# Eight PSUM banks as one tile in place of four tiles of two banks, in a fused attention and phase-mixing kernel

## The chip, the cores and the metric

The kernel runs on one core of a Trainium2 chip. The metric is the device time of one execution in microseconds. Five queues run side by side, each in its own order: PE (TensorE, matrix multiplications and transposes into PSUM), DVE (VectorE), ACT (ScalarE), POOL (GpSimd, here elementwise work in SBUF and DMA issue) and SP (SyncE, here DMA issue). They are kept in step by semaphores: an instruction waits until the counters of other engines and of DMAs have reached certain values. PSUM has eight banks of 512 float32 per partition.

## The reference

Inputs are q, k and v of shape (4, 8, 768, 64) and four matrices. Attention is causal; heads 0, 2 and 6 see all earlier keys, the other five see the first four keys and a window of 64. Its output x (768 x 512 per batch element) goes through a phase mixing over the sequence and a channel step:

```
scores = where(mask, q @ k.T / 8, -1e9);  a = softmax(scores);  x = a @ v      # heads side by side
theta = x @ w_theta
y = w_tok_r @ (x * cos(theta)) + w_tok_i @ (x * sin(theta))
u = x + y
out = u + max(u @ w_ch, 0)
```

## The kernel before

The whole program is one list of steps, `ORDER`, written out by hand; no scheduler moves anything. A step such as `mx.1.3.0.0` names a helper and its arguments, and each helper issues its instructions on a fixed engine (or the one that the letter D, A or P at the end of the step names). Each engine runs its part of the list in list order. The waits between engines are placed by the tile framework when the program is built, from the tiles and parts of tiles that each instruction reads and writes.

Work goes by batch element (first argument), in 128-row tiles of the sequence, and steps of two or three batch elements are interleaved. The steps, with the PSUM banks that they use as their last number:

- `lf`, `lq`, `lv`, `lt`, `lw` load q and k, v, the token matrices and the two weights; q, k and the token matrices go by POOL's queue, v and the first q and k by SP's.
- `tq` turns a pair of heads of q or k on PE into one bank (lines 252 and 255), and `eq` copies it out to SBUF by ACT (line 259) or DVE (line 261). `xp`/`xe` do the same for x, `wt`/`we` for the token matrices (line 437), `up`/`ue` for u (line 423).
- `pm` puts the additive mask into one or two banks (lines 290, 294), `s` adds the scores (line 319), `e` takes the exponential of both banks in one ACT instruction (line 349, or 346 for one bank), and `m` masks by multiplication on DVE (lines 359 to 371).
- `av` multiplies with the values into two banks (line 406), `n` normalises both (lines 411, 413).
- `th` makes theta for two row tiles in two banks (line 446), `tr` takes cosine and sine of both (lines 450, 451), `z` multiplies with x on DVE or POOL (lines 458, 459).
- `mx` accumulates a third of the token mixing of one row tile in one bank (line 463, 4 matmuls; three steps fill the bank), `u` adds x to it on DVE (line 469).
- `xd` and `ud` transpose x and u by DMA from SP's queue (line 418), `ch` multiplies u with w_ch into one bank (line 473), `o` is the last step on DVE (line 476), `st` stores. `w` issues matmuls whose result nobody reads (line 432).

The eight banks are numbered 0 to 7. They are held by four tiles of two banks each; bank b is half b % 2 of tile b // 2, so that 0 and 1, 2 and 3, 4 and 5, 6 and 7 share a tile. `one(bank)` gives one bank, `two(bank)` a pair that starts with an even number:

```
    def one(bank):
        return banks[bank // 2][:, bank % 2]

    def two(bank):
        return banks[bank // 2]
```

Of the kernel before, what the change touches and what calls it, by code (L numbers as in the profile page):

```python
# [8 lines left out]
F32 = mybir.dt.float32  # L9
# [99 lines left out]
def kernel(ctx: ExitStack, tc: tile.TileContext, q, k, v, is_retrieval, n_sink, window, w_theta, w_tok_r, w_tok_i, w_ch, out):  # L109
# [9 lines left out]
    psum = ctx.enter_context(tc.tile_pool(name="psum", bufs=1, space=bass.MemoryType.PSUM))  # L119
    ctx.enter_context(tc.manual_schedule())  # L120

    def new(name, shape, dtype=BF16):
        return sb.tile(shape, dtype, name=name)
# [24 lines left out]
    u, uT = [new(f"u{n}", [128, DM]) for n in range(U_BUFS)], [new(f"uT{n}", [128, KD, 128]) for n in range(U_BUFS)]  # L148
    ot = [new(f"ot{n}", [128, DM], F32) for n in range(OT_BUFS)]
    rr = [new(f"rr{n}", [128, 8], F32) for n in range(2)]  # L150
    banks = [psum.tile([128, 2, 512], F32, name=f"bank{n}") for n in range(4)]

    def one(bank):
        return banks[bank // 2][:, bank % 2]
# [405 lines left out]
```

## Time and profile before

| | us |
|---|---|
| median of 3 runs | 195.82 |
| the three runs | 193.15, 195.82, 196.24 |
| the profiled execution | 194.51 |
| its span, first to last instruction | 192.8 |
| PE busy | 171.1 |
| DVE busy | 138.1 |
| ACT busy | 114.0 |
| POOL busy | 59.3 |

The profile is that of one execution. Busy times are those of each engine's own work; weight loads of PE (PEld) run beside its matmuls. In a timeline row the bracket at the end gives how long the engine was idle before the row and whose work ended that: "0.71 <-DVE u L469" is 0.71 us until DVE's instruction of line 469, which writes u, had finished. The names leave buffer numbers out, so which bank a row works on is read from the list of steps. Line numbers are those of the kernel before.

### The profile page before, as it was taken

The page shows a single profiled execution, that of the slowest core. Times are in us where ns is not written, and L with a number is a line of the kernel's source. Part 1 is how long each engine was busy: PE and PEld are TensorE (multiplying, and loading weights), DVE is VectorE, ACT ScalarE, POOL GpSimd, SP SyncE. Part 2 cuts the span into 40 slices and gives each one's busy share as a digit, 9 for nine tenths or more (in the row PEclk, how much of TensorE's full clock was granted, in tenths as well). Part 3 has the DMA queues.
Part 4 walks back from the last instruction along what each step waited for, and adds up shares of the span by engine and source line. Part 5 has one row for each costly group of instructions (what it writes and reads, how often), then busy time and mean ns, then how long its engine had stood idle before and what let it go on. Part 6 is the DMA issues. An engine that isn't in the chain of part 4 may idle for free.

```text
span 192.8 us, 4430 instructions
## 1 busy us (share of the span) xinstructions
PE 171.1 (89%) x1821; PEld 95.6 (50%) x1821; DVE 138.1 (72%) x253; ACT 114.0 (59%) x132; POOL 59.3 (31%) x99
## 2 busy tenths in 40 slices
PE   5585978999898999989989989998899999998970
PEld 5353466755554476534445665443346644443430
DVE  4523854999687975689979988999778838825442
ACT  4596799899888908468997036788653066100000
POOL 7314954626254504351822316160000000400000
PEclk9889999999999999999999999999999999999999
DMA  5998899945999989699899998851421555116454
GB/s 169 259 203 186 121 200 200 203 89 83 155 195 185 186 121 136 135 156 238 103 181 220 141 192 146 195 137 27 126 95 27 114 107 136 54 58 196 130 199 154
DMA packets 62227, 28.72 MB, mean 149 GB/s; under 512 B 48384, under 2 KB 59136, under 8 KB 62208
## 3 DMA queue, kind: packets, MB, share of 16 engines
q1 hardware_dynamic: 51808, 19.54, 46.7%
q0 software_dynamic: 10400, 8.92, 32.1%
q8 instruction: 14, 0.23, 0.5%
q14 instruction: 5, 0.04, 0.1%
HBM read 25.69 MB, written 6.29 MB: 166 GB/s over the span
## 4 chain that ended last, share of the span: by engine, by line
PE 64%; DVE 20%; ACT 9%; DMA 2%; issue 2%; DVEq 0%; SPq 0%
PE bank L463 28%; PE bank L473 10%; PE bank L446 8%; PE bank L319 5%; PE bank L406 5%; DVE ot L476 4%; PE bank L255 3%; DVE qT L261 3%; ACT P L349 3%; DVE kT L261 3%; DVE u L469 3%; DMA early<-in_k_dram 2%; DVE early L458 2%; PE bank L437 2%; ACT kT L259 1%
## 5 line engine op out<-in xcount | busy, mean ns | idle before, releaser
L349 ACT ACTIVATE P<-bank 128x1024 bf16<-128x1024 f32 (+2 forms) x64 | 56.8, 944 | 9.2 <-PE bank L319 8.6
L463 PE MATMUL bank<-zr,wtokTr 128*128 128x512 bf16 x72 | 27.3, 379 | 2.1 <-DVE u L469 1.2
L463 PE MATMUL bank<-early,wtokTr 128*128 128x512 bf16 x72 | 27.3, 379 | 1.5 <-DVE u L469 0.9
L463 PE MATMUL bank<-early,wtokTi 128*128 128x512 bf16 x72 | 27.3, 379 | 0.0
L463 PE MATMUL bank<-zi,wtokTi 128*128 128x512 bf16 x72 | 27.3, 379 | 0.0
L473 PE MATMUL bank<-w_ch_sb,uT 128*128 128x512 bf16 x96 | 24.0, 379 | 1.3 <-DVE ot L476 0.6
L463 PEld LDWEIGHTS <-wtokTi 128*128 128x128 bf16 x144 | 14.0, 98 | 17.6 <-issue 4.7
L463 PEld LDWEIGHTS <-wtokTr 128*128 128x128 bf16 x144 | 14.0, 97 | 16.9 <-issue 2.4
L476 DVE SCALAR_TENSOR_TENSOR ot<-bank,u 128x512 f32<-128x512 f32 x24 | 16.0, 685 | 6.4 <-PE bank L473 4.3
L319 PE MATMUL bank<-qT,kT 64*128 64x128 bf16 (+2 forms) x240 | 20.0, 256 | 0.2 <-ACT kT L259 0.2
L450 ACT ACTIVATE ct<-bank,half_pi 128x1024 f32<-128x1024 f32 x12 | 13.4, 1115 | 10.2 <-PE bank L446 8.0
L406 PEld LDWEIGHTS <-P 128*128 128x128 bf16 x472 | 16.6, 97 | 4.9 <-issue 1.5
L261 POOL CAST vt<-st_v 128x512 bf16<-128x512 f32 x12 | 9.8, 823 | 27.1 <-DMA st_v<-in_v_dram 26.3
L406 PE MATMUL bank<-vt,P 128*128 128x65 bf16 x372 | 16.9, 193 | 1.1 <-ACT P L349 1.0
L371 DVE TENSOR_TENSOR P<-P,m_stream 128x1024 bf16<-128x1024 bf16 (+3 forms) x27 | 14.3, 557 | 2.6 <-ACT P L349 2.6
L458 POOL TENSOR_TENSOR early<-early,st 128x512 bf16<-128x512 bf16 x3 | 3.4, 1160 | 41.5 <-issue 35.7
L473 PEld LDWEIGHTS <-uT 128*128 128x128 bf16 x96 | 9.1, 97 | 11.9 <-issue 2.1
L319 PEld LDWEIGHTS <-kT 64*128 64x128 bf16 x240 | 11.0, 96 | 7.5 <-issue 5.9
L469 DVE TENSOR_TENSOR u<-early,bank 128x512 bf16<-128x512 bf16 x12 | 8.1, 683 | 8.4 <-PE bank L463 7.0
L261 DVE COPY qT<-bank 128x768 bf16<-128x768 bf16 x9 | 8.4, 951 | 6.8 <-PE bank L255 3.0
L261 POOL COPY kO<-kT 128x320 bf16<-128x320 bf16 (+3 forms) x18 | 5.3, 322 | 23.0 <-DVE kT L261 14.1
L451 ACT ACTIVATE st<-bank 128x1024 f32<-128x1024 f32 x12 | 12.2, 1018 | 0.0
(90 smaller groups left out, 293.8 us busy)
## 6 DMA issues: line engine op xcount, KB each, us to landing
st_v<-in_v_dram SPq DMA_DIRECT2D x24, 256.0 KB, 6.9
out_dram<-ot SPq DMA_DIRECT2D x24, 256.0 KB, 2.3
qb<-in_q_dram POOLq DMA_DIRECT2D x14, 192.0 KB, 7.9
kb<-in_k_dram POOLq DMA_DIRECT2D x14, 192.0 KB, 7.8
wtok<-in_moe_w_tok_r_dram POOLq DMA_DIRECT2D x6, 192.0 KB, 6.3
wtok<-in_moe_w_tok_i_dram POOLq DMA_DIRECT2D x6, 192.0 KB, 6.4
early<-in_q_dram SPq DMA_DIRECT2D x2, 384.0 KB, 4.9
early<-in_k_dram SPq DMA_DIRECT2D x2, 384.0 KB, 5.9
```

Source lines behind the costliest of these rows:

```text
L261: (nc.vector if eng == "D" else nc.gpsimd).tensor_copy(o, i)
L319: nc.tensor.matmul(*mms[g], start=not seeded, stop=True, skip_group_check=True)
L349: nc.scalar.activation(o, two(bank)[:, :, :o.shape[2]], AF.Exp, scale=scale)
L371: nc.vector.tensor_tensor(o, o, mk, ALU.mult)
L406: nc.tensor.matmul(o, l, r, start=(m == 0), stop=True, skip_group_check=True)
L446: nc.tensor.matmul(two(bank)[:, y], xT[b % 2][:, kk, i * 128:(i + 1) * 128], w_theta_sb[:, kk], start=(kk == 0), stop=(kk == KD - 1))
L450: nc.scalar.activation(ct[n], two(bank), AF.Sin, bias=half_pi)
L451: nc.scalar.activation(st[n], two(bank), AF.Sin)
L463: nc.tensor.matmul(one(bank), wtokT[n][:, s, t * 128:(t + 1) * 128], z[b % 2][:, s], start=(s == 0 and n == 0), stop=(s == NB - 1 and n == ...
L469: nc.vector.tensor_tensor(u[ui(b, t)], x[b % 2][:, t], one(bank), ALU.add)
L473: nc.tensor.matmul(one(bank), uT[ui(b, t)][:, kk], w_ch_sb[:, kk], start=(kk == 0), stop=(kk == KD - 1))
L476: nc.vector.scalar_tensor_tensor(ot[(NB * b + t) % OT_BUFS], one(bank), 0.0, u[ui(b, t)], ALU.max, ALU.add)
```

## The change

One tile of eight banks is allocated, and the four names are views of two banks each. Addresses, shapes, the list of steps and every instruction stay as they are:

```
-    banks = [psum.tile([128, 2, 512], F32, name=f"bank{n}") for n in range(4)]
+    big = psum.tile([128, 8, 512], F32, name="big")
+    banks = [big[:, 2 * n:2 * n + 2] for n in range(4)]
```

What moves is where the framework puts waits. In the program built from the kernel before, 79 of the waits between engines name an instruction that touches only the other bank of the same tile (28 where DVE waits for PE, 20 PE for DVE, 17 between ACT and PE, 14 between ACT and DVE). In the program of the changed kernel there is none: every wait for PSUM names an instruction on the same bank. What an instruction is sure to come after is in no place more than before. Written out, the waits on other engines and on DMAs are PE 304 before and 319 now, DVE 243 and 251, ACT 144 and 148, POOL 112 and 110, SP 159 and 158; the instructions that raise a counter are PE 183 and 190, DVE 205 and 213, ACT 122 and 128.

Two places in the built programs. A row is line, operation, out<-in and shape, with the counters that it waits for; `bank_128` is the tile of banks 0 and 1, `bank_130` that of 4 and 5. First PE in the third quarter of the program, the steps `tq.3.k.1.1`, `tq.3.k.3.4` and `tq.3.q.1.5`: before,

```order
L255 LDWEIGHTS kb
L255 MATMUL bank_128<-ident,kb 64x128 [waits Activation_49]
...
L255 LDWEIGHTS kb [waits DMASW7_49]
L255 MATMUL bank_130<-ident,kb 64x128 [waits Activation_49]
...
L255 LDWEIGHTS qb [waits DMASW6_49]
L255 MATMUL bank_130<-ident,qb 64x128
```

and now,

```order
L256 LDWEIGHTS kb
L256 MATMUL big<-ident,kb 64x128 [waits Activation_49]
...
L256 LDWEIGHTS kb [waits DMASW7_49]
L256 MATMUL big<-ident,kb 64x128 [waits DVE_49]
...
L256 LDWEIGHTS qb [waits DMASW6_49]
L256 MATMUL big<-ident,qb 64x128 [waits Activation_49]
```

The turn of k into bank 4 waited for ACT, which copies bank 5 out (`eq.3.q.0.5.A`), and the turn of q into bank 5 then needed no wait. Now the first waits for DVE, which copies bank 4 out (`eq.3.k.0.4.D`), and the second for ACT.

Second DVE at the end of the program, the steps `u.3.5.0` to `o.3.3.1`, all on the tile of banks 0 and 1 but one: before,

```order
L469 TENSOR_TENSOR u_115<-early_100,bank_128 128x512 [waits PE_49]
L261 COPY uT_121<-bank_128 128x512 [waits PE_49]
L476 SCALAR_TENSOR_TENSOR ot_122<-bank_128,u_112 128x512 [waits DMAHW5_49,DVE_49]
L476 SCALAR_TENSOR_TENSOR ot_124<-bank_129,u_114 128x512 [waits DMAHW7_49,DVE_49,PE_49]
L476 SCALAR_TENSOR_TENSOR ot_125<-bank_128,u_115 128x512 [waits DMAHW0_49,DVE_49,PE_49]
L476 SCALAR_TENSOR_TENSOR ot_123<-bank_128,u_113 128x512 [waits DMAHW2_49]
```

and now,

```order
L470 TENSOR_TENSOR u_115<-early_100,big 128x512 [waits PE_49]
L262 COPY uT_121<-big 128x512 [waits PE_49]
L477 SCALAR_TENSOR_TENSOR ot_122<-big,u_112 128x512 [waits DMAHW5_49,DVE_49]
L477 SCALAR_TENSOR_TENSOR ot_124<-big,u_114 128x512 [waits DMAHW7_49,DVE_49,PE_49]
L477 SCALAR_TENSOR_TENSOR ot_125<-big,u_115 128x512 [waits DMAHW0_49,DVE_49,PE_49]
L477 SCALAR_TENSOR_TENSOR ot_123<-big,u_113 128x512 [waits DMAHW2_49,PE_49]
```

The two last rows were both held by one wait for PE, in front of the first of them, for the last matmul of the program. Now each waits for PE on its own, the first for the matmuls of its own bank. The first row waits for PE as before, but for the mix in its own bank and no longer for the channel step in the other one, which the row can't show, since it leaves out the counter's value.

## The prediction

> **What bounds the kernel now.** First the page of the profiled execution: busy time, then the chain of work that ended last.
>
> ```profile
> span 192.8 us, 4430 instructions
> PE 171.1 (89%) x1821; PEld 95.6 (50%) x1821; DVE 138.1 (72%) x253; ACT 114.0 (59%) x132; POOL 59.3 (31%) x99
> PE 64%; DVE 20%; ACT 9%; DMA 2%; issue 2%; DVEq 0%; SPq 0%
> ```
>
> TensorE (PE) is busy for 171.1 of 192.8 us, yet only 64% of the chain is its: 20% runs through VectorE (DVE) and 9% through ScalarE (ACT). The chain changes engine wherever PE waits until a PSUM bank has been read, or a reader waits until PE has filled one. This execution took 194.51 us, 1.71 us more than its span and 0.7% below the median of 195.82 us. Then busy time by stage (columns: stretch, its length, then PE, PEld, DVE, ACT, POOL busy with counts, clock, DMA):
>
> ```profile
> 6.00:21.50 15.50, 10.88 (x146) 7.13 (x148) 5.84 (x17) 11.21 (x14) 5.72 (x13) 0.89 0.98 190
> 21.50:30.00 8.50, 7.27 (x133) 4.81 (x126) 5.32 (x14) 8.36 (x12) 5.88 (x9) 1.00 1.16 199
> 36.00:49.00 13.00, 12.36 (x162) 7.04 (x159) 12.59 (x16) 11.95 (x14) 6.61 (x8) 1.00 0.71 116
> 83.00:94.00 11.00, 10.56 (x78) 4.95 (x78) 10.33 (x14) 8.96 (x10) 4.48 (x6) 1.00 1.22 164
> 94.00:109.00 15.00, 14.40 (x185) 8.21 (x184) 13.45 (x34) 10.30 (x13) 5.64 (x9) 1.00 1.14 170
> 140.00:174.00 34.00, 34.00 (x273) 17.48 (x273) 22.73 (x44) 11.95 (x12) 2.28 (x2) 1.00 0.32 81
> ```
>
> From 140 to 174 us PE is never idle, from 21.5 to 30 ACT is full, from 36 to 49 DVE is: nothing that shortens waits pays much there. From 6 to 21.5 us no engine is full. They wait for each other, and the question for every such wait is whether the two instructions share a bank or only a tile.
>
> **The change, part by part.** No instruction is added, removed or moved, on any queue, and none grows. What goes are the 79 waits in which one engine waits for work on the other bank of a two-bank tile. No wait holds anything longer than in before, since each instruction is held by a subset of what held it. So the sum runs over stalls that such waits end, up to where the next wait ends last. Bank numbers are those of the order (last number of a step).
>
> *6 to 21.5 us.* Rows of the timeline (start, duration, engine, line, and in brackets the idle time before and what ended it):
>
> ```profile
> 7.44 0.49 PE L252 MATMUL bank<-ident,kb 128*128 128x128 bf16 x6 [2.07 <-ACT qT L259]
> 7.97 0.80 ACT L259 COPY kT<-bank 128x768 bf16<-128x768 bf16 x1 [0.58 <-PE bank L252]
> 10.33 0.82 PE L252 MATMUL bank<-ident,qb 128*128 128x128 bf16 x6
> 12.38 0.96 DVE L261 COPY qT<-bank 128x768 bf16<-128x768 bf16 x1 [2.58 <-PE bank L432]
> 13.38 0.55 PE L432 MATMUL bank<-ident 128*128 128x128 bf16 x7 [0.57 <-DVE qT L261]
> 15.39 0.22 PE L290 MATMUL bank<-n_causal,ident 128*128 128x128 bf16 x1 [0.79 <-DVE kT L261]
> 16.59 0.38 ACT L346 ACTIVATE P<-bank 128x256 bf16<-128x256 f32 x1 [1.79 <-PE bank L255]
> 17.71 0.86 PE L255 MATMUL bank<-ident,qb 128*64 128x128 bf16 x24 [0.84 <-ACT kT L259]
> 19.35 0.53 PE L255 MATMUL bank<-ident,kb 128*64 128x128 bf16 x12 [0.78 <-DVE qT L261]
> 20.26 1.02 ACT L349 ACTIVATE P<-bank 128x1024 bf16<-128x1024 f32 x1 [0.85 <-PE bank L319]
> ```
>
> All five PE rows with a bracket wait for the other bank: k.0's turn (bank 1) for the copy out of bank 0; `w.7.7` for the copy out of 6; the seed `pm.0.5.3` for 2; q.2's turn into 3 for 2; k.3's turn into 2 for 3. DVE's copy at 12.38 reads bank 6, whose turn ended at 10.33 + 0.82 = 11.15, and waits for warm-up matmuls in bank 7. ACT carries this stage into its full stretch, so I count on ACT. The first stall gives it 0.55 of its 0.58 us. The next two, in series on PE, give 0.57 + 0.79; with 0.55 that is 1.91, and ACT's row at 16.59 comes at 14.68, when ACT is indeed free (16.59 - 1.79 - 0.55 = 14.25). The last two free PE by 0.84 + 0.78, of which ACT can use its idle 0.85 at 20.26. Sum 1.91 + 0.85 = 2.8 us; at least 1.9, at most 0.58 + 1.79 + 0.85 = 3.2.
>
> The clock in this stage is not the change's, but the shorter pause might touch it:
>
> ```profile
> 8.83 1.57 PE L319 MATMUL bank<-qT,kT 64*128 64x256 bf16 x12 [0.20 <-ACT kT L259]
> 10.00:11.00 1.00, 1.00 (x10) 0.56 (x6) 0.00 (x0) 0.99 (x2) 0.54 (x1) 0.50 1.28 192
> ```
>
> PE had half its clock there (0.50), after the 2.07 us pause; I take the same again, 0. The Trainium skill ("TensorE: Matmul & The Clock Gate", What's actually happening) says that about 3.4 us with too little PE activity, in a free-running window, halve the clock. By that rule the pause, shorter by 0.70, may leave the clock up and the 12 matmuls might take half of 1.57 us: 0.8 us more saved. The trace agrees with a halved clock and can't show the window.
>
> *30 to 60 us.*
>
> ```profile
> 30.46 0.81 PE L446 MATMUL bank<-w_theta_sb,xT 128*128 128x512 bf16 x3 [0.49 <-DVE xT L261]
> 44.20 1.82 DVE L261 COPY qT<-bank 128x768 bf16<-128x768 bf16 x2 [0.38 <-ACT kT L259]
> 57.83 0.80 ACT L259 COPY wtokTr<-bank 128x768 bf16<-128x768 bf16 x1 [0.48 <-PE bank L437]
> 58.66 1.13 DVE L261 COPY wtokTi<-bank 128x768 bf16<-128x768 bf16 x2 [1.65 <-ACT wtokTr L259]
> ```
>
> Bank 2 of theta waits for a copy out of 3 (0.49); DVE as reader of one bank waits for ACT as reader of its neighbour at 44.20 (0.38) and 58.66, where it sits through ACT's copy of 0.80. Sum 1.6, all on the path; at least 0.8, because DVE has only 13.00 - 12.59 = 0.41 us to give from 36 to 49; at most 0.49 + 0.38 + 1.65 = 2.5.
>
> *60 to 140 us.*
>
> ```profile
> 72.68 0.38 PE L463 MATMUL bank<-zr,wtokTr 128*128 128x512 bf16 x1 [0.71 <-DVE u L469]
> 82.99 1.02 PE L473 MATMUL bank<-w_ch_sb,uT 128*128 128x512 bf16 x4 [0.52 <-DVE kT L261]
> 86.64 0.69 DVE L476 SCALAR_TENSOR_TENSOR ot<-bank,u 128x512 f32<-128x512 f32 x1 [0.67 <-PE bank L463]
> 100.08 0.38 PE L463 MATMUL bank<-early,wtokTr 128*128 128x512 bf16 x1 [0.60 <-DVE u L469]
> 113.49 0.53 PE L255 MATMUL bank<-ident,kb 128*64 128x128 bf16 x12 [0.88 <-ACT qT L259]
> 134.59 0.38 PE L463 MATMUL bank<-zr,wtokTr 128*128 128x512 bf16 x1 [0.47 <-DVE u L469]
> 138.32 0.69 DVE L476 SCALAR_TENSOR_TENSOR ot<-bank,u 128x512 f32<-128x512 f32 x1 [0.30 <-PE bank L463]
> 139.06 0.38 PE L463 MATMUL bank<-zr,wtokTr 128*128 128x512 bf16 x1 [0.78 <-DVE ot L476]
> ```
>
> PE at 72.68 fills bank 1 and waits for the reader of 0, at 82.99 the reverse: 0.71 + 0.52 = 1.2 us, at least 0.7. Then DVE is nearly full too (0.67 us free from 83 to 94). At 86.64 `o.0.5.0` waits for a mix in bank 1 and heads a run of DVE work; at 100.08 and 113.49 PE waits for the neighbour: 0.67 + 0.60 + 0.88 = 2.15. I take 2.0; at least 0.9 (the last stall alone), at most 2.2. From 132 on 0.47, and 0.30 of the 0.78: that wait stays, for `o.1.5.2` in the same bank, which itself loses only its 0.30 for bank 3: 0.8; at least 0.5, at most 0.47 + 0.78 = 1.25.
>
> *140 us to the end.*
>
> ```profile
> 175.21 0.38 PE L463 MATMUL bank<-early,wtokTr 128*128 128x512 bf16 x1 [0.49 <-DVE ot L476]
> 182.84 0.38 PE L463 MATMUL bank<-early,wtokTi 128*128 128x512 bf16 x1
> 184.12 0.69 DVE L469 TENSOR_TENSOR u<-early,bank 128x512 bf16<-128x512 bf16 x1 [1.11 <-PE bank L473]
> 184.86 0.40 PE L423 MATMUL bank<-ident,u 128*128 128x128 bf16 x4 [0.78 <-DVE u L469]
> 186.37 1.89 PE L473 MATMUL bank<-w_ch_sb,uT 128*128 128x512 bf16 x8 [0.25 <-DVE ot L476]
> 188.29 1.29 DVE L476 SCALAR_TENSOR_TENSOR ot<-bank,u 128x512 f32<-128x512 f32 x2 [1.38 <-PE bank L473]
> ```
>
> At 175.21 bank 1 waits for `o.2.3.0` (bank 0): 0.5. The add `u.3.5.0` needs the mix that ended at 182.84 + 0.38 = 183.22 and waits until 184.12 for `ch.3.2.1`: it starts 0.86 earlier, the turn behind it by 0.75 of PE's 0.78, `ch.3.5.0` by 0.25 more. At the very end both finishing adds wait for the last matmul; now the first (1.29 / 2 = 0.65) runs beside it: 0.6. Sum 1.6; at least 1.2, at most 1.8.
>
> *What comes in its place.* There are 27 more waits (PE 15, DVE 8, ACT 4). A hand-over takes 0.05 us (`u` ends at 184.81, the turn starts at 184.86), so at most 27 x 0.05 = 1.35; one that is already met should cost little: 0.3. Next late are the transposing DMAs, which PE's channel matmuls need:
>
> ```profile
> DMA to landing us min/median/max: 2.4/2.5/8.9
> ```
>
> Each starts earlier with its `u`, but where DMAs are dense (1.14 to 1.22 in the last column but one, 83 to 109 us) earlier work doesn't make them faster, and the longest took 6.4 us more than the median: 0.7. Together -1.0, between 0 and -3.
>
> The skill has a rule against the change as well: by the same page (The cost: per-tile semaphore tail) matmuls' semaphore increments serialize at about 26 ns each. PE gets 7 more signalling instructions: an estimate of 0.2 us, by which the saving below would be 9.3. No row here separates such a tail.
>
> *Sum.* 2.8 + 1.6 + 1.2 + 2.0 + 0.8 + 0.5 + 1.6 - 1.0 = 9.5 us: 194.51 - 9.5 = 185.0 for the profiled execution, and 195.82 / 194.51 of that, 186.3, for a median; I say **186 us**.
>
> **The rivals.**
>
> *Absorbed.* Only the two ends, where no engine is full, keep their gain, at its lower bounds: 1.9 + 1.2 = 3.1, so 191.4, or 192.7 as a median. For it: from 83 to 109 us PE and DVE are both over 89% busy, so one's gain meets the other's work. Against it: most stalls there sit on PE itself, which is on the path. Chance 0.12.
>
> *Slower.* From 83 to 117 us loads for the next batch, asked for earlier, run into the transposes of `u`, and PE stops at `ch`. One landing late by 8.9 - 2.5 = 6.4 us leaves 9.5 - 6.4 = 3.1 saved (192.7); three in series lose 19.2 and give 205.5. It decides beyond 9.5 + 3.9 = 13.4 us lost. Against it: the loads and the transposes move earlier together. Chance 0.03.
>
> *The change doesn't do what it says*: eight banks held as one, any reader waiting for any matmul. From 6 to 21.5 us alone, ACT and PE in turn would take 11.21 + 10.88 = 22.1 us in place of 15.5: over 201 us in all. The built program has no such wait: 0.
>
> **How the numbers follow.** The forecast has 0.85. All terms at their lower ends give 6.5 - 3 = 3.5, at their upper ends 12.7; not all err together, so 5.5 to 12.5, or 183.3 to 190.3 as medians. The three runs of before reach from 193.15 to 196.24, so a median may sit 1% lower still: 182 to 191. About 2% (3.9 us) is what a measurement here can tell from no change. Faster by more: the forecast less its low edge, 0.84; within: 0.13; slower: 0.03.
>
> **What would show it.** Right: the brackets above at 13.38, 72.68, 100.08 and 175.21 are gone; no add of L469 waits for a channel matmul of L473; ACT's full stretch begins about 2.8 us earlier; PE stays at about 171 us busy in a span near 183. Wrong: the same idle time in front of PE with other releasers (DMA, or readers of the same bank), or stalls that go while L473 waits for `uT` in their place.

## The result, and the profile after

| | before | after |
|---|---|---|
| median of 4 runs, us | 195.34 (193.15 to 196.24) | 185.87 (185.3 to 186.6) |
| profiled execution, us | 194.51 | 185.3 |
| its span, us | 192.8 | 183.3 |

After takes 0.9553 of the time of before (95% interval 0.9457 to 0.9649). Beside later kernels, on another chip, it took 187.78 us (186.16 to 188.66), 0.9631 of before (0.9557 to 0.9705); after's own median moves by 2 us between chips, so kernels are compared below within one chip where less than that matters. On some chips part of the executions of a kernel form a second group that is 1% to 3% slower; medians, ranges and ratios here and below are those of the faster group (the 187.96 us that an expectation quotes is the median of all).

The page of after (busy time; the chain that ended last; 25 of its 1821 matmul records are missing, so that PE's 166.9 is somewhat low):

```profile
span 183.3 us, 4404 instructions
PE 166.9 (91%) x1796; PEld 94.7 (52%) x1821; DVE 135.8 (74%) x253; ACT 113.3 (62%) x132; POOL 57.8 (32%) x99
PE 64%; DVE 12%; DMA 10%; ACT 8%; issue 2%; POOL 1%; SPq 1%; POOLq 0%; DVEq 0%
```

DVE's share of the chain fell from 20% to 12%, that of DMAs rose from 2% to 10%. The engines wait for each other less, and transfers have become what is late. By stage (same columns as before), with the cut 2.8 us earlier, at 18.70 in place of 21.50, where the forecast puts the start of ACT's full stretch:

```profile
6.00:18.70 12.70, 11.65 (x151) 7.50 (x152) 6.63 (x19) 11.40 (x15) 3.97 (x9) 1.00 1.09 218
18.70:27.00 8.30, 7.01 (x124) 4.77 (x124) 5.87 (x13) 8.18 (x13) 5.73 (x10) 1.00 1.02 156
```

ACT's instruction that starts at 21.54 in before starts at 17.91 here, so that the stretch begins 3.63 us earlier. The 1.00 in the clock column (third from the end) says little for the first microseconds: the clock records of this trace begin at 9.6 us, and the column shows 1.00 where there is none. The experiment with a seam comes back to this.

At the end, the add `u.3.5.0` (first row) no longer waits 1.11 us for a channel matmul but 0.17 us for its own mix, and three finishing adds run in a row where the last two used to wait 1.38 us for PE:

```profile
175.65 0.69 DVE L470 TENSOR_TENSOR u<-early,big 128x512 bf16<-128x512 bf16 x1 [0.17 <-PE big L464]
177.17 2.08 DVE L477 SCALAR_TENSOR_TENSOR ot<-big,u 128x512 f32<-128x512 f32 x3
179.42 0.69 DVE L477 SCALAR_TENSOR_TENSOR ot<-big,u 128x512 f32<-128x512 f32 x1 [0.17 <-PE big L474]
```

What has come in place of the old stalls stands in the waits of after (who <- for what: us in total, times, longest):

```profile
PEld L474 <- DMA uT<-u: 3.3, 3, 2.6
PEld L447 <- DMA xT<-x: 1.6, 1, 1.6
PE big L464 <- DVE wtokTi L262: 2.0, 1, 2.0
```

Since no instruction changed its place on an engine, the n-th weight load of PE (or the n-th instruction of ACT or DVE) is the same work in both traces. Start in before less start in after is the lead of after at that point:

| instruction | start before | start after | lead | since the row above |
|---|---|---|---|---|
| PE, scores (L319 before) | 24.13 | 20.50 | 3.63 | +3.63 |
| ACT, copy of kT | 43.37 | 38.58 | 4.79 | +1.16 |
| PE, scores | 45.75 | 43.09 | 2.66 | **-2.13** |
| PE, mix | 62.84 | 58.22 | 4.62 | +1.96 |
| ACT, sine | 86.79 | 80.51 | 6.28 | +1.66 |
| PE, mix | 88.03 | 83.81 | 4.22 | **-2.06** |
| PE, values | 104.84 | 99.81 | 5.03 | +0.81 |
| PE, values | 108.70 | 104.33 | 4.37 | **-0.66** |
| PE, theta | 120.44 | 114.35 | 6.09 | +1.72 |
| PE, mix | 125.37 | 120.55 | 4.82 | **-1.27** |
| PE, channel | 148.60 | 141.93 | 6.67 | +1.85 |
| PE, mix | 172.75 | 165.95 | 6.80 | +0.13 |
| PE, mix | 179.96 | 172.43 | 7.53 | +0.73 |
| DVE, last add | 188.90 | 179.42 | 9.48 | +1.95 |

The gains add up to 15.60 us, and 6.12 are given back at four places. The experiments ask three things: are the waits between banks the cause, do the gains of the stretches add, and what takes the 6 us back?

### The profile page after: what moved, and what is told of

The parts are those of the page before. It is cut to its first block, busy times and chain, and to the rows that moved or that the text cites. A ratio compares the mean times of both kernels' runs of the same rounds, so it can differ in the third digit from the quotient of the medians.

```text
span 183.3 us, 4404 instructions
## 1 busy us (share of the span) xinstructions
PE 166.9 (91%) x1796; PEld 94.7 (52%) x1821; DVE 135.8 (74%) x253; ACT 113.3 (62%) x132; POOL 57.8 (32%) x99
## 4 chain that ended last, share of the span: by engine, by line
PE 64%; DVE 12%; DMA 10%; ACT 8%; issue 2%; POOL 1%; SPq 1%; POOLq 0%; DVEq 0%
PE big L464 28%; PE big L474 9%; PE big L447 7%; PE big L320 6%; PE big L407 6%; DMA st_v<-in_v_dram 5%; ACT P L350 4%; DVE kT L262 3%; PE big L256 3%; DMA xT<-x 2%; DMA early<-in_k_dram 2%; PE big L438 2%; DVE qT L262 2%; DVE early L459 2%; DVE zr L459 1%
## 5 line engine op out<-in xcount | busy, mean ns | idle before, releaser
L350 ACT ACTIVATE P<-big 128x1024 bf16<-128x1024 f32 (+2 forms) x64 | 56.7, 947 | 9.5 <-PE big L320 8.6
L464 PE MATMUL big<-zi,wtokTi 128*128 128x512 bf16 x70 | 26.5, 379 | 0.8 <-issue 0.6
L464 PE MATMUL big<-early,wtokTi 128*128 128x512 bf16 x69 | 26.2, 379 | 0.3 <-issue 0.2
L464 PE MATMUL big<-early,wtokTr 128*128 128x512 bf16 x69 | 26.2, 380 | 0.2
L464 PE MATMUL big<-zr,wtokTr 128*128 128x512 bf16 x64 | 24.3, 380 | 2.1 <-DVE wtokTi L262 2.0
L474 PE MATMUL big<-w_ch_sb,uT 128*128 128x512 bf16 x94 | 23.6, 379 | 2.5 <-DVE early L459 2.4
L320 PE MATMUL big<-qT,kT 64*128 64x128 bf16 (+2 forms) x240 | 19.9, 255 | 0.4 <-DVE kT L262 0.4
L477 DVE SCALAR_TENSOR_TENSOR ot<-big,u 128x512 f32<-128x512 f32 x24 | 16.2, 687 | 5.2 <-PE big L474 4.4
L451 ACT ACTIVATE ct<-big,half_pi 128x1024 f32<-128x1024 f32 x12 | 13.4, 1115 | 10.2 <-PE big L447 7.2
L407 PE MATMUL big<-vt,P 128*128 128x65 bf16 x372 | 17.1, 193 | 1.1 <-ACT P L350 1.0
L474 PEld LDWEIGHTS <-uT 128*128 128x128 bf16 x96 | 8.8, 98 | 12.9 <-DMA uT<-u 3.3
L470 DVE TENSOR_TENSOR u<-early,big 128x512 bf16<-128x512 bf16 x12 | 8.1, 684 | 5.4 <-PE big L464 5.2
```

Of the source, the lines that this page charges most:

```text
L320: nc.tensor.matmul(*mms[g], start=not seeded, stop=True, skip_group_check=True)
L350: nc.scalar.activation(o, two(bank)[:, :, :o.shape[2]], AF.Exp, scale=scale)
L407: nc.tensor.matmul(o, l, r, start=(m == 0), stop=True, skip_group_check=True)
L451: nc.scalar.activation(ct[n], two(bank), AF.Sin, bias=half_pi)
L464: nc.tensor.matmul(one(bank), wtokT[n][:, s, t * 128:(t + 1) * 128], z[b % 2][:, s], start=(s == 0 and n == 0), stop=(s == NB - 1 and n == ...
L474: nc.tensor.matmul(one(bank), uT[ui(b, t)][:, kk], w_ch_sb[:, kk], start=(kk == 0), stop=(kk == KD - 1))
```

## The experiments

**Tiles of four banks.** Is it the waits, or does a larger tile save something by itself?

```diff
-    big = psum.tile([128, 8, 512], F32, name="big")
-    banks = [big[:, 2 * n:2 * n + 2] for n in range(4)]
+    big = [psum.tile([128, 4, 512], F32, name=f"big{n}") for n in range(2)]
+    banks = [big[n // 2][:, 2 * (n % 2):2 * (n % 2) + 2] for n in range(4)]
```

> The eight banks as two tiles of four. In the built program a tile of four is held as a whole, so that a reader of any of its banks waits for matmuls in the other three: 252 waits for another bank against 79 in before and none in after. Theory (these waits are what costs the time): by before's 9.5 net and some 15 us gross for 79 waits, 0.12 to 0.2 us each, slower than before by 173 x 0.12 to 0.2 = 21 to 35 us: 216 to 230 us. Rival (fewer, larger tiles save something by themselves, such as the handling of tiles): between after and before, 186 to 195 us.

Measured: 268.93 us (267.65 to 269.47), 1.377 of before (1.3709 to 1.3831). Page of this kernel, and its busy time from 140 to 174 us, where PE is never idle in before:

```profile
span 266.9 us, 4412 instructions
PE 190.2 (71%) x1795; PEld 103.3 (39%) x1821; DVE 138.7 (52%) x253; ACT 115.7 (43%) x132; POOL 59.7 (22%) x99
140.00:174.00 34.00, 24.61 (x289) 14.00 (x293) 21.68 (x39) 11.28 (x12) 6.71 (x15) 0.95 0.67 118
```

PE works 24.61 of 34 us there (the same time, though not the same work), and 71% of the whole span in place of 89%. A larger tile saves nothing: the direction is the theory's and excludes the rival. The size is not. 268.9 - 195.2 (before on this chip) is 74 us for 173 more waits, 0.43 us each, against the 0.12 to 0.2 expected. Not all of it need be waiting: PE is also busy 19.1 us longer than in before (190.2 and 171.1) for the same matmuls, at a granted clock of 0.917 over this profile against 0.990 there. How much of the 74 us that makes is open; an execution at 0.949 took 267.65 us, only 1.3 us less. A price per wait taken from four pairs does not carry over to two groups of four; my reading, not tested, is that fewer free banks are left to run ahead into.

**A seam at 33 us.** The PSUM pool is closed behind the step `n.0.5.6` and opened again, with one tile of eight (t) or four of two (f) on either side; the step `wt.0.0.0` is written behind `n.0.5.6` for this.

```diff
+        if step == "n.0.5.6":
+            held.close()
+            held, banks[:] = psum_tiles("psb", True)   # False in the second variant
```

> The changed kernel, with its PSUM pool closed behind the step n.0.5.6 (near 33 us of before) and a second one opened, one tile of eight banks on either side of that seam. It is the control for the next two. Theory (the saving is the waits between neighbouring banks that fall away, stretch by stretch, less what the DMAs and the other engines give back): the seam alone costs nothing that can be measured, 185.3 to 187.5 us. Rival (something else than the waits, for instance the clock in the first stage or how instructions are placed): no forecast of its own; a control above 189 us would make the next two unreadable.

> Four tiles of two banks up to the seam, one tile of eight behind it: the waits of the first 33 us are back, all later ones stay away. Before and after, laid instruction against instruction, stand 3.6 to 3.8 us apart at 21 to 24 us. Theory (the gains of the stretches add): slower than the control by about 3.8 us, 190 us, and the lag against before starts near 0 at 24 us and grows behind the seam as after's does. Rival (absorbed: what is gained early is lost again where the next loads and PE's and VectorE's full stretch set the pace): within 1 us of the control, 186 to 187 us.

> One tile of eight up to the seam, four tiles of two behind it: only the first 33 us are free of the waits. Theory (the gains add): the lead of 3.8 us at 24 us stays to the end, the rest of the saving (9.5 - 3.8 = 5.7 us) is lost: 191 to 192 us. Rival (absorbed): the early lead is worn off before the end, since the same stalls stand behind the seam as in before: 194 to 195.5 us.

| tiles before / behind the seam | median, us | range | of before |
|---|---|---|---|
| one / one (control) | 187.69 | 185.48 to 187.71 | 0.9579 (0.9474 to 0.9685) |
| four / one | 189.93 | 189.02 to 191.1 | 0.9735 (0.9667 to 0.9803) |
| one / four | 194.58 | 193.68 and 195.47, two runs | before itself 195.15 us (195.12 to 195.26) |

The control stands 0.2 us above the 185.3 to 187.5 expected. Bringing the waits of the first 33 us back costs 2.2 us by medians (189.93 - 187.69): below the 3.8 expected, above the rival's 1. The intervals overlap, so the size stays rough. The traces differ by more than the waits, too. With four tiles of two, this kernel is 1.53 us ahead of before at 11.88 us of before, and stays there (1.52 at 24 us). Of these, 0.83 are there at 7.44 us, where PE waits for the copy of the first k load, which landed that much earlier, and 0.70 come while before ran at half clock. Windows, with the clock third from the end, first before, then this kernel:

```profile
8.00:10.00 2.00, 1.80 (x18) 1.07 (x15) 1.16 (x6) 1.37 (x2) 0.28 (x1) 0.50 1.25 227
```

```profile
8.00:10.00 2.00, 1.70 (x22) 1.07 (x22) 0.45 (x4) 1.67 (x3) 0.82 (x1) 1.00 1.30 227
```

After has 0.38 us from that load and nothing from the clock. Its clock column shows 1.00 there, but its 12 score matmuls take as long as the same 12 in before at 0.50 (1.57 us), not as long as here. The row of after, then that of this kernel:

```profile
8.08 1.57 PE L320 MATMUL big<-qT,kT 64*128 64x256 bf16 x12
```

```profile
8.00 0.88 PE L325 MATMUL psa_bank<-qT,kT 64*128 64x256 bf16 x12 [0.45 <-ACT kT L265]
```

So the bank waits of the first stage are worth about 3.63 - 0.38 = 3.25 us in after's trace. That the medians show only 2.2 is not explained.

With four tiles behind the seam the early lead is there (3.84 us at 33 us of before) and is gone at the end; the time is nearer the rival's than the 191 to 192 expected. Weight loads of this kernel:

```profile
31.27 0.10 PEld L443 LDWEIGHTS <-wtok 128*128 128x128 bf16 x1 [1.28 <-issue]
87.84 0.55 PEld L479 LDWEIGHTS <-uT 128*128 128x128 bf16 x4 [2.56 <-DMA uT<-u]
```

The seam itself takes 1.84 us (lead 3.84 to 2.00; the first PE instruction on the new pool waits for the readers of the old one), some 0.4 go until 44 us, and the last 2.0 at one instruction, `ch.0.0.0` at 87.84, which waits 2.56 us for a transposing DMA: lead 1.59 ahead of it, -0.46 behind. This is where after gives 2.06 us back too. It does not follow that an early lead is worth nothing past this point: the kernel of the next experiment, which comes there without a lead, loses 1.53 us at the same DMA. With a seam that takes half of the lead itself, this run does not decide whether the gains add.

**The end alone.** Before with two channel matmuls put into other banks, so that no pair at the end is shared.

```diff
-... ch.3.2.1 ... o.3.2.1 ... ch.3.3.1 ... o.3.3.1
+... ch.3.2.4 ... o.3.2.4 ... ch.3.3.6 ... o.3.3.6
```

> Before, four tiles of two, with two channel matmuls of the last token tiles put into other banks: ch.3.2.1 into bank 4 and ch.3.3.1 into bank 6, so that no pair holds both them and what the next reader needs. Three of the 79 waits go, all behind 183 us. Theory: the end's term (1.6 us forecast; by the two traces the lag grows there from 7.60 to 9.48, 1.9 us) belongs to these waits alone: 1.4 to 1.9 us faster than before. Rival (the end is bound by the matmuls and the last adds in series, and the lag there came from what lies ahead): under 0.5 us.

Measured: 194.31 against 195.37 us, ratio 0.9928 (0.9882 to 0.9973), so 1.4 us faster by the ratio (0.5 to 2.3): the theory, though the time alone only just excludes the rival. DVE's rows behind 184 us, which in before waited 1.11 and 1.38 us for PE's L473:

```profile
184.74 0.69 DVE L469 TENSOR_TENSOR u<-early,bank 128x512 bf16<-128x512 bf16 x1 [0.25 <-PE bank L463]
187.29 1.94 DVE L476 SCALAR_TENSOR_TENSOR ot<-bank,u 128x512 f32<-128x512 f32 x3 [0.36 <-DMA out_dram<-ot]
```

Against before the lead goes from -1.49 to +0.34 there, 1.83 us, as in after (1.95). (The 1.49 were lost at `ch.0.0.0` near 87 us, where the two programs are the same: here its DMA took 7.3 us to land and PE waited 2.04 us for it. What happens at that place differs between executions of one order.) The end's term belongs to three waits on a neighbouring bank, and new bank numbers for two steps get it without joined tiles.

**The first give-back, at 36 to 46 us.** In after, DVE's two copies of kO (first fence; 1.69 us is the first of them) run beside two `zi` steps of GpSimd (POOL, second):

```profile
36.31 1.76 DVE L262 COPY kO<-kT 128x320 bf16<-128x320 bf16 x2
```

```profile
35.58 2.29 POOL L459 TENSOR_TENSOR zi<-x,st 128x512 bf16<-128x512 bf16 x2
```

The first copy ends at 36.31 + 1.69 = 38.00, GpSimd's second step at 35.58 + 2.29 = 37.87. The experiment moves two `zi` steps to DVE.

```diff
-... z.0.1.i.1.P ... z.0.2.i.0.P
+... z.0.1.i.1.D ... z.0.2.i.0.D
```

> After, with two of the zi steps (z.0.1.i.1 and z.0.2.i.0) on VectorE instead of GpSimd. In after VectorE's copy of kO takes 1.69 us at 36 us beside GpSimd's two zi steps, against 0.26 in before where GpSimd was idle then, and zi 1.64 against 0.68; the lead over before falls there from 4.7 to 2.9 us. Theory (the two engines slow each other when both work in SBUF): the copy is back near 0.3 us and the zi steps near 0.7, VectorE takes up 2 x 0.7 us more of its own, so 0 to 1.5 us faster at 46 us, of which the end may keep less. Rival (the copy's length comes from its own form or from DMA traffic): the copy stays at 1.69, and the kernel is slower by 1.4 us at 46 us.

DVE's rows of this kernel, both kO copies in one and two `zi` steps in the other:

```profile
35.91 0.33 DVE L262 COPY kO<-kT 128x320 bf16<-128x320 bf16 x2
37.28 1.28 DVE L459 TENSOR_TENSOR zi<-x,st 128x512 bf16<-128x512 bf16 x2
```

In before GpSimd was not idle at this pair either: the first copy took 0.26 us, but the second, beside a `zi` of GpSimd, 1.12. Without GpSimd beside it the pair of copies takes 0.33 us in place of 1.76, a `zi` step 0.64 in place of 1.64: the mechanism is the theory's. It also delayed the copy out of wtokTi behind it, for which PE waits 2.0 us in after. How much is lost depends on how the two meet: in the second profile of after the two copies took 1.56 us, in three kernels below, with the same order at this place, 1.18, 1.17 and 1.19. The time, 185.13 us (184.1 to 185.77), or 0.9478 of before (0.9412 to 0.9544), can't be told from after's 0.9553 and 0.9631. Against after's first profile it is 1.95 us ahead at 44 us and 0.87 at the end, but that is not the moved steps' doing: the next kernel, whose order is after's up to 73 us, is 1.89 us ahead at 44 us and 0.83 at the end. In it and two more with that order the first copy takes 1.10 to 1.12 us and DVE's next `zi` 0.68, where after's first profile has 1.69 and 1.64. The difference of 1.55 is what that profile loses more here: 2.13 us against 0.60 in each of the three. So the give-back is the two engines meeting, and its size is a matter of the execution. Moving the steps brings it to 0.36 us, and then costs: from 62.84 to 86.79 us of before this kernel gains 0.71 us where after gains 1.66.

**The second give-back, at 83 us.** After's weight load for `ch.0.0.0`; the issues around that transposing DMA on GpSimd's and SP's queue; its time to landing (minimum, median, maximum of one):

```profile
83.15 0.54 PEld L474 LDWEIGHTS <-uT 128*128 128x128 bf16 x4 [2.57 <-DMA uT<-u]
75.78 0.76 POOL L228 DMA_DIRECT2D kb<-in_k_dram  x1
76.54 1.43 POOL L228 DMA_DIRECT2D qb<-in_q_dram  x2
75.93 1.23 SPq L419 DMA_TRANSPOSE uT<-u  x1
DMA to landing us min/median/max: 7.2/7.2/7.2
```

The same DMA in before:

```profile
80.64 1.23 SPq L418 DMA_TRANSPOSE uT<-u  x1
DMA to landing us min/median/max: 5.9/5.9/5.9
```

It landed at 86.5, and PE came to it at 86.97, so 0.4 us later. Now it is issued 4.71 us earlier, but PE gets there 6.3 us earlier, and the landing takes 1.3 us more. First attempt: that DMA ahead of the load of v.

```diff
-... tr.1.0.6 lv.2.4 ch.0.2.3 o.0.3.2 st.0.1 th.1.1.4 ud.0.0 ...
+... tr.1.0.6 ud.0.0 lv.2.4 ch.0.2.3 o.0.3.2 st.0.1 th.1.1.4 ...
```

> After, with the transposing DMA of the second turn of u (ud.0.0) written ahead of the next batch's loads (lv.2.4) instead of behind them. In after ch.0.0.0 waits 2.57 us at 83 us for that DMA, which takes 7.2 us from issue to landing while the loads of q and k go out at 75.8 to 77.3 us. Theory (the transposing DMA queues behind the loads' packets): the wait goes, 1 to 2.5 us faster than after: 183.5 to 185 us. Rival 1 (DMA engines are full there whatever the order, and the landing stays where it is): within 0.4 us of after. Rival 2 (the loads come later and the next batch waits): slower than after by up to 1 us.

Measured 185.55 us (184.48 to 187.21), 0.9532 of before (0.9464 to 0.9599): after's time, and above the 183.5 to 185 expected. The transposing DMA, ahead of the loads, lands after 2.5 us and is no longer waited for, but PE and DVE stand just as long:

```profile
81.68 0.59 PE L474 MATMUL big<-w_ch_sb,uT 128*128 128x512 bf16 x2 [2.81 <-DVE ot L477]
80.93 0.69 DVE L477 SCALAR_TENSOR_TENSOR ot<-big,u 128x512 f32<-128x512 f32 x1 [3.16 <-DMA out_dram<-ot]
```

DVE needs a buffer of `ot` whose store, issued at 75.03 behind a load of v, lands 5.8 us later (2.3 at the median of before), and PE needs the bank that DVE would read. It is not this DMA that is slow but whatever stands behind the loads. So the next kernels, on one chip, take loads away: two loads of q and k for the last batch are issued later, or all eight are left out, or the later loads are joined with what was tried above.

```diff
 # two loads later; the next kernel leaves out all eight lq.3 steps
-... lv.2.0 lq.3.k.1 z.1.0.r.2.D ... z.1.0.i.0.D lq.3.q.2 z.1.1.i.0.D ...
+... lv.2.0 z.1.0.r.2.D ... z.1.0.i.0.D z.1.1.i.0.D ...
-... e.2.4.4 lq.3.k.2 ... ud.1.0 lq.3.q.0 ...
+... e.2.4.4 lq.3.k.1 lq.3.k.2 ... ud.1.0 lq.3.q.2 lq.3.q.0 ...
```

> The changed kernel once more, beside the next three on one chip: 185 to 187.5 us. All theories expect the same; it is what the others are held against, and its profile tells which waits come back in every execution: the 2.57 us of ch.0.0.0 for the transposing DMA at 83 us should (1.5 us or more), VectorE's copy of kO of 1.69 us at 36 us may not, since it hangs on how GpSimd's zi step and the copy happen to meet.

> After, with two loads of q and k for the last batch (lq.3.k.1 and lq.3.q.2, 192 KB each) issued behind those of GpSimd's steps that follow near 86 us, instead of at 75.8 to 77.3 us. Theory (what is gained ahead of 83 us is given back there to DMA engines that are full: whichever transfer is behind the loads lands late): two loads fewer in the way, ch.0.0.0 waits under 1 us, 1 to 2 us faster than after. Rival (the loads of v, 256 KB each, fill the DMA engines alone): ch.0.0.0 waits as before, within 0.5 us of after.

> After without any load of q and k for the last batch (eight loads of 192 KB, 1.5 MB); the last batch is computed from the batch before it, all instructions of the engines are the same. It measures what the DMA traffic between 75 and 110 us costs this kernel at all. Theory (some 4 of the 6 us that after gives back go to DMAs that land late): 180 to 182.5 us, and no wait over 1 us for uT or for ot's store. Rival (the give-back lies in the engines' own work, and PE and VectorE are full there): 184.5 us or more.

> Late_q3, and with it: the transposing DMA ud.0.0 and the store st.0.1 ahead of lv.2.4, and the two zi steps on VectorE. In the run with ud.0.0 moved alone, ch.0.0.0's wait of 2.57 us for uT went, but VectorE then waited 3.16 us for a store of ot; with the zi steps on VectorE the copy of kO was 0.26 us. Theory: neither wait is left, 1.5 to 3.5 us faster than after: 182 to 184.5 us. Rival (a third transfer is late in their place): within 1 us of after.

| kernel | median, us | range | of before | wait of `ch.0.0.0` |
|---|---|---|---|---|
| after | 187.78 | 186.16 to 188.66 | 0.9631 (0.9557 to 0.9705) | 3.34 |
| two loads later | **183.15** | 182.32 to 184.14 | 0.9404 (0.9349 to 0.9460) | 0.60 |
| without the eight loads | 181.8 | 180.19 to 182.59 | 0.9324 (0.9252 to 0.9396) | 1.65 |
| later, and DMA, store and `zi` moved | 184.16 | 183.3 to 185.0 | 0.9457 (0.9401 to 0.9513) | none for `uT` |

The wait in after and with two loads later, and the time to landing of that DMA in after, with two loads later, without the loads:

```profile
83.80 0.11 PEld L474 LDWEIGHTS <-uT 128*128 128x128 bf16 x2 [3.34 <-DMA uT<-u]
79.70 0.57 PEld L474 LDWEIGHTS <-uT 128*128 128x128 bf16 x4 [0.60 <-DMA uT<-u]
DMA to landing us min/median/max: 7.7/7.7/7.7
DMA to landing us min/median/max: 4.9/4.9/4.9
DMA to landing us min/median/max: 6.0/6.0/6.0
```

After's median is 0.3 us above its expectation of 185 to 187.5; both waits came back, the copy of kO with 1.49 us.

Busy time from 78 to 86 us, in one fence each: after (its second profile, as above), two loads later, without the loads.

```profile
78.00:86.00 8.00, 4.84 (x33) 2.14 (x31) 6.33 (x9) 5.63 (x6) 0.61 (x1) 1.00 1.30 176
```

```profile
78.00:86.00 8.00, 7.22 (x63) 3.38 (x62) 7.22 (x10) 6.76 (x7) 3.88 (x6) 1.00 1.15 179
```

```profile
78.00:86.00 8.00, 6.53 (x55) 3.05 (x54) 6.50 (x10) 5.73 (x6) 1.86 (x2) 1.00 1.15 167
```

PE works 4.84 of 8 us in after and 7.22 with two loads out of the way. The change of the lead over before at the four places where after gives back, from one profile of each (the same pairs of instructions as in the table above):

| from / to, us of before | after, first | after, again | two loads later | without the loads |
|---|---|---|---|---|
| 43.37 / 45.75 | -2.13 | -1.93 | -0.60 | -0.60 |
| 86.79 / 88.03 | -2.06 | -2.84 | -0.13 | -1.14 |
| 104.84 / 108.70 | -0.66 | -0.91 | 0.00 | 0.00 |
| 120.44 / 125.37 | -1.27 | -1.34 | -1.00 | +0.06 |
| lead at the end | 9.48 | 6.67 | 12.45 | 13.00 |

At the second and third place moving two loads is enough; the fourth goes only when all eight are out, so these three hang on the loads. Two things stay open. Without the eight loads `ch.0.0.0` still waits 1.65 us, against the expected "no wait over 1 us": the loads of v are still there, and its DMA takes 6.0 us. And each load of q or k also takes 0.7 us of GpSimd's time to issue, which no run separates from its traffic; at the second place it is the landing that got shorter. Moving two loads is worth more than the theory gave it: 4.6 us by medians (187.78 - 183.15), where 1 to 2 were expected for the second place alone. The profiles give 5.09 - 1.13 = 4.0 for the three; the first place, ahead of every load that was moved, differs by 1.3 more, which is GpSimd and DVE meeting otherwise. Both profiles of after lose about 2 us there and three of other kernels with the same order 0.60; whether that is so in most runs is open. Leaving the loads out brings another 1.4 us, so that at most 6.0 hang on them. The combination did not beat its simplest part. Its profile points at the `zi` steps on DVE for most of the 1.0 us: from 45.75 to 86.79 it gains 2.43 us on before, as the kernel with those steps alone (2.07), against 3.21 with only the loads moved. The fastest kernel here that loads everything is after with two loads written later: 183.15 us.

**The same loads in before.** Is this cost the change's doing, or was it always there?

> Before, four tiles of two, with the same two loads of q and k (lq.3.k.1 and lq.3.q.2) moved back as in late_q3, which took after from 187.96 to 183.15 us (4.8 us). Theory (the change itself brought the loads in front of the transposing DMA that PE needs at 83 us; in before the loads go out at 81.35 us, behind that DMA's issue at 80.64, and PE does not wait there for a DMA): under 1.5 us faster than before, 194 to 195.5 us. Rival (the loads cost that much in either kernel, and the give-back of after is something else): 4 to 5 us faster, 190.5 to 191.5 us.

Measured 195.9 against 195.04 us for before on this chip, ratio 1.0045 (1.0004 to 1.0086): nothing gained, and the 194 to 195.5 expected is missed on the slow side. In before's order the time does not hang on these two loads as after's does, so the change brought most of this cost to light. It was not free of it: with the end apart, in that same order, PE waits at `ch.0.0.0` as well, and with the loads moved it still waits 0.66 us.

```profile
88.88 0.55 PEld L473 LDWEIGHTS <-uT 128*128 128x128 bf16 x4 [2.04 <-DMA uT<-u]
```

That PE's waits for neighbouring banks hide the loads in before is my reading, not tested.

## Why the prediction held, and where it did not

**The time.** 186 us was forecast and 185.87 measured, 185.0 for the profiled execution and 185.3 measured. That it came so close is luck: gains were forecast at 10.5 (9.5 + 1.0) and are 15.6 us, the return at 1.0 and is 6.1.

**Term by term** (forecast, its bounds, and the lead gained between rows of the table):

| stretch of before, us | forecast | measured |
|---|---|---|
| 6 to 21.5 | 2.8 (1.9 to 3.2) | 3.63, without the earlier load 3.25 |
| 30 to 60 | 1.6 (0.8 to 2.5) | 1.16 + 1.96 = 3.12 |
| 60 to 83 | 1.2 (from 0.7) | 1.66 |
| 83 to 132 | 2.0 (0.9 to 2.2) | 0.81 + 1.72 = 2.53 |
| 132 to 140 | 0.8 (0.5 to 1.25) | 1.85 |
| 140 to 182 | 0.5 | 0.13 + 0.73 = 0.86 |
| end | 1.6 (1.2 to 1.8) | 1.95 |
| in its place | -1.0 (0 to -3) | -6.12 |

Signs and places are right for all stretches; in five of them the gain is above the upper bound, by 0.05 to 0.62 us. The step that failed on this side is the bound by stalls: each stretch was given only idle time that the quoted rows show in brackets, and that was too little in two ways. Between 30 and 60 us PE has waits in before that the prediction left out:

```profile
48.68 0.53 PE L255 MATMUL bank<-ident,qb 128*64 128x128 bf16 x12 [0.45 <-DVE kT L261]
56.96 0.83 PE L437 MATMUL bank<-ident,wtok 128*128 128x128 bf16 x12 [0.25 <-DVE wtokTi L261]
59.84 0.49 PE L437 MATMUL bank<-ident,wtok 128*128 128x128 bf16 x6 [0.65 <-DVE wtokTi L261]
```

In after's second profile PE is idle less than 0.1 us in front of each, and its lead grows there by 0.37, 0.41 and 0.81 us. And at 139.06 only 0.30 of the 0.78 us were counted, since that wait is for a reader of the same bank and "stays". It went whole: the matmul starts without a pause and PE's lead grows by 0.95, to 4.22, because DVE, whose lead at its reading of that bank is 4.45, is done in time.

**What comes in its place** is the term that was wrong, at twice its worst bound. The mechanism was named (transposing DMAs that PE's channel matmuls need), its size was not: 0.7 us was about a tenth of the 6.4 us by which the longest landing exceeded the median, taken with the reason that "each starts earlier with its `u`". So it does, but PE's need came forward by 6.3 us and the issue by 4.71, and the landing grew from 5.9 to 7.2 us. In the two profiles of after the one wait is 2.57 and 3.34 us, and moving two loads gave 4.6 us back. Unforeseen was DVE beside GpSimd at 36 us, though before has the sign of it, a pair of kO copies that ends (41.63) with GpSimd's `zi` (41.60):

```profile
40.33 1.30 DVE L261 COPY kO<-kT 128x320 bf16<-128x320 bf16 x2
```

```profile
40.44 1.16 POOL L458 TENSOR_TENSOR zi<-x,st 128x512 bf16<-128x512 bf16 x1 [2.49 <-ACT st L451]
```


**The rivals.** *Absorbed* does not hold for the whole change. For its first part alone it is open: free banks up to 33 us and pairs behind end near before's time, but half of the lead goes to the seam. *Slower* had the right mechanism and place, with one long wait instead of three, at 2.6 to 3.3 us instead of 6.4. *The change doesn't do what it says* was given 0, rightly; tiles of four show what being held as a whole costs, 74 us.

**What would show it.** The brackets at 13.38, 72.68, 100.08 and 175.21 have gone, and ACT starts its full stretch 3.6 us earlier. For the adds of L469 (L470 in after) the trace names:

```profile
  PE big L464: 8.1, 10
  PE big L474: 0.2, 1
```

One wait of 0.17 us is still put down to a channel matmul; the program has none, and releasers are inferred. PE's 171 us was too high. The kernel with one DMA moved, whose profile has all 1821 matmuls, shows:

```profile
span 182.4 us, 4429 instructions
PE 168.8 (93%) x1821; PEld 94.9 (52%) x1821; DVE 135.4 (74%) x253; ACT 113.4 (62%) x132; POOL 60.0 (33%) x99
```

Of the two signs of being wrong, the second came true in part: the stalls went, and L474 waits for `uT` in their place, though not for as long.

**The clock rule.** The prediction took nothing for the clock, and that was right: before and after both run the 12 score matmuls in 1.57 us, though after's clock column shows 1.00. By the Trainium skill's rule ("TensorE: Matmul & The Clock Gate", What's actually happening), that about 3.4 us with too little PE activity halve the clock, 0.8 us more might have been saved. No run here shows the tiles or the pauses deciding it: the kernel with four tiles up to the seam, with before's tiles and waits in this stage, ran them in 0.88 us.

## What to carry to other kernels

When waits between engines are removed, the transfers do not get faster with them: compare how much earlier each DMA is issued with how much earlier it is needed, and move loads with slack behind those without, which here brought 4.6 us beside the 7.4 of the change on the same chip (195.18 - 187.78); by the traces up to 1.3 of the 4.6 may not be theirs. Look in the built program for waits on work that shares a tile but not a bank; joining tiles helps only if the parts are then told apart, and made this kernel 1.38 times as slow where they were not. Check a forecast that comes out right by its parts, instruction against instruction: two errors of 5 us cancelled here.

## What the runs showed of the hardware

VectorE and GpSimd hold each other up in SBUF for whole instructions. A 128x320 bf16 copy with a small one behind it took 0.33 us alone and 1.76 us when it met two GpSimd steps; the large one ended 0.13 us after GpSimd's second. The Trainium skill says so ("SBUF — State Buffer", SBUF: two separate sides): the shared port pair is an exclusive lock, held for the whole instruction by whichever comes first of a GpSimd instruction and a VectorE one in a two-port mode or with two SBUF inputs. The trace agrees, and adds that one VectorE copy may have to let two GpSimd instructions pass (36.31 to 38.00 us, across the end of the first).

A transposing DMA that takes 2.5 us at the median of before takes much longer when loads of 192 and 256 KB are under way. The one for `ch.0.0.0` took 5.9 us in before, 7.3 with the end apart, 7.2 and 7.7 in after, 4.9 with two of the loads moved, 6.0 without the eight loads of q and k, and 2.5 when issued ahead of the loads. A 256 KB store next to it waits in the same way (5.8 us).

Early in the kernel PE runs at half clock in many executions: the 12 score matmuls near 8 us take 1.57 us in before at 0.50, the same in after, and 0.88 with four tiles up to the seam. The clock column can't be trusted ahead of a trace's first clock record, where it shows 1.00; what the same matmuls take tells more.
